# Chained attention and two mixtures of experts: a score burst moved next to another, a first-logits step moved, flags in bf16, prefix counts on TensorE

## The chip, the cores and the metric

One core of one Trainium2 chip runs the whole program. The metric is the device time of one execution in microseconds (us); lower is better. PE is TensorE's matmul side and PEld its weight loads, DVE is VectorE, ACT is ScalarE, POOL is GpSimd, SP is SyncE, which here issues most of the DMAs. PSUM is the memory into which TensorE writes its products.

## The reference

Three layers follow each other. The sizes are batch 8, 8 heads, 576 positions, head size 64, 32 packed queries `p`; 8 experts with 512 inputs and 1024 hidden units.

```python
p_packed = sm_attn(p, k, v)            # softmax(p k^T / 8) v
out = sm_attn(q, p_packed, p_packed)   # softmax(q p_packed^T / 8) p_packed
x = out.transpose(0, 2, 1, 3).reshape(B * S, H * D)
# layer 1: every row goes to its best of 8 experts
idx = argmax(x @ w_gate); g = softmax(x @ w_gate)[idx]
x = g * (relu(x @ w1[idx]) @ w2[idx])
# layer 2: only rows with x @ w_skip > 0, added to x
out = x; out[do] = x[do] + g * (relu(x[do] @ w1[e]) @ w2[e])
```

## The kernel before, in words

The kernel is one program for TensorE above all. For each batch b it has a **main pass** `gen_M(b)` (from line 756): the batch is taken with one expert of layer 1, in two halves of 288 positions. A half is stage 1 (8 hidden blocks f, 6 matmuls each, line 728) and stage 2 (4 output blocks t, 24 matmuls each, line 749). Each product is taken as three matmuls, since both factors are split in a high and a low fp32r part: `hh` (ACT, line 733) and `hl` (DVE, line 734) are the parts of the hidden values, `W2h` and `W2l` those of the second weights, `A2h` and `A2l` those of the attention weights, `Q1h` and `Q1l` those of the first weights multiplied by the packed attention values. An output block t leaves PSUM by ACT (line 765) in the first half and by DVE, times the gates `gB`, in the second (line 767, the *sink*). The second stage of batch 7's first half is gated as well. The rows that belong to another expert than the batch's are done afterwards as *extra units* (`gen_x`, with `x_flags` finding them) and layer 2 as *items* (`e_item`) with a *small unit* beside them (`gen_pick` chooses its rows).

The work of the other batches goes between the steps of the main pass. `Weave` counts the 48 steps of a main pass (one f of stage 1, or 6 matmuls of stage 2) and calls a *side generator* when its place comes: a side is (generator, number of pieces n, a, b) and its pieces stand evenly between the fractions a and b of the pass. A piece that uses TensorE (marked `TE`) is let in only at every fourth step, and only one of each side at a step. So the tuple of numbers sets the order of every engine's queue. The lines that set it in a pass of batch b:

```python
plan = ((NS, 0.06, 0.18, TE), (NT, 0.18, 0.477), (8, 0.5, 1.06))   # b = 1..5
plan = ((NS, 0.06, 0.17, TE), (NT, 0.17, 0.33), (NR, 0.34, 0.52))  # b = 6
sides.append((pre, 5, 0.88, 1.0, TE))
sides.append((w2, 4, 0.76, 1.1))
```

The sides that matter here:

- `gen_S(b+2)`, the **scores**: 16 small matmuls of keys with the packed queries (helper at line 385, output `s`, 64x32 tiles of the array), row maxima `mx` on DVE (line 407), `nm`, four exponentials on ACT (line 417), then the transposes `at` on PE (line 434) of those results, copied by ACT (`aT`).
- `gen_pre(b+1)`: loads of the first weights and the **q products** of them (line 385, output `q`, four PSUM outputs of 128x512, the same 64x32 tiles), each split by ACT (`Q1h`, line 623) and DVE (`Q1l`, line 624).
- `gen_w2(b+1)`: four loads and splits of the second weights (`W2h` on ACT, `W2l` on POOL).
- `gen_R(b)`: the first logits (line 580) and their routing, in the end `csA` (line 588), from which `x_flags` (line 966) finds with 10 fp32 matmuls (line 970) which extra units are needed.
- `gen_post`: the second logits (line 793).

PSUM is one pool of eight banks, handed out in turn (`mt`, line 241): a bank is written again when the product that stood in it eight calls earlier has been read.

At batch 7, `gen_x` prepares an extra unit beside the first half of the main pass: four gate products `xro` on DVE (line 1040), then the transposes `xt` on PE (line 1046). After the second half the program loads the register `cA` (line 1509) in every engine and branches on it.

Of the kernel before, what the change touches and what calls it, by code (L numbers as in the profile page):

```python
# [15 lines left out]
ALU = mybir.AluOpType  # L16
# [102 lines left out]
def attn_moe_kernel(ctx, tc, q, k, v, p, wg, w11, w12, w21, w22, out):  # L119
# [18 lines left out]
    def ct(name, shape, dt=F32, fill=None, eng=None):  # L138
        t = const.tile(shape, dt, name=name)
        if fill is not None:  # L140
            (eng or nc.vector).memset(t, fill)
        return t
# [5 lines left out]
    iot = ct("iot", [128, 128])  # L148
    pid = ct("pid", [128, 1])
    E8 = ct("E8", [128, E])  # L150
    M5 = ct("M5", [128, 5, 2, NXP])
    once = ct("once", [128, 5, 32])
    tri = ct("tri", [128, 128])
    ones = ct("ones", [128, 128])
# [566 lines left out]
    def stage1(lh, ll, rh, rl, kt, hh, hl, hf=None):  # L721
        n_, nr = hh.shape[2], rh.shape[2]
        for f in range(8):
            ps = mt("h")
            n = 0
            for t in range(kt):
                for l, r in ((lh, rh), (lh, rl), (ll, rh)):
                    nc.tensor.matmul(  # L728
                        out=ps[:, 0:nr], lhsT=l[:, t, 128 * f:128 * f + 128], rhs=r[:, t, :],
                        start=(n == 0), stop=(n == 3 * kt - 1),  # L730
                    )
                    n += 1
            nc.scalar.activation(out=hh[:, f, :], in_=ps[:, 0:n_], func=ACTF.Relu)  # L733
            nc.vector.scalar_tensor_tensor(  # L734
                out=hl[:, f, :], in0=ps[:, 0:n_], scalar=0.0, in1=hh[:, f, :].bitcast(F32),
                op0=ALU.max, op1=ALU.subtract,
            )
            if nr > n_:
                nc.vector.tensor_scalar(out=hf[:, f, :], in0=ps[:, n_:nr], scalar1=0.0, scalar2=None, op0=ALU.max)
            yield  # L740
# [224 lines left out]

    def x_flags():
        f0 = mt("f0")
        for z in range(2):
            for s in range(5):
                nc.tensor.matmul(  # L970
                    out=f0[0:NXP, B * z:B * z + B], lhsT=M5[:, s, z, :], rhs=csA[:, s, :], start=(s == 0), stop=(s == 4)
                )
        FL = X["FL"]
        Fv = FL.rearrange("p (b z) -> p b z", z=2)
        nc.vector.tensor_scalar(
            out=Fv, in0=kmA[0:NXP, :].unsqueeze(2).to_broadcast([NXP, B, 2]), scalar1=-1.0, scalar2=float(E),
            op0=ALU.mult, op1=ALU.add,
        )
        nc.vector.tensor_tensor(out=FL, in0=FL, in1=valx[:, :, 2], op=ALU.not_equal)
        nc.vector.scalar_tensor_tensor(  # L980
            out=Fv, in0=f0[0:NXP, 0:2 * B].rearrange("p (z b) -> p b z", z=2), scalar=0.0, in1=Fv,
            op0=ALU.is_gt, op1=ALU.mult,
        )
        nc.tensor.matmul(out=f0[0:32, 64:64 + 2 * B], lhsT=ones[0:NXP, 0:32], rhs=FL, start=True, stop=True)
        nc.vector.tensor_reduce(
            out=X["cnt"], in_=f0[0:32, 64:64 + 2 * B].rearrange("p (b z) -> p b z", z=2), op=ALU.add, axis=AX.X
        )
# [44 lines left out]
                out=EB["W2"][:, :, 128 * t:128 * t + 128], in_=w12[dsn(ex, 1), t].rearrange("o p f c -> p (o f) c")  # L1032
            )

    def gen_x(X):
        li = X["li"]
        A2g, bd, xt, hr, hx, ro, yx = (X[n] for n in ("A2", "bd", "xt", "hq", "hx", "rq", "y"))
        for hp in range(4):
            r = slice(32 * hp, 32 * hp + 32)
            nc.vector.tensor_tensor(  # L1040
                out=bd[r, :, hp, :], in0=A2g[r], in1=X["gB"][r].unsqueeze(1).to_broadcast([32, 2, UW]), op=ALU.mult
            )
        yield
        ps = mt("xt")
        for x in range(2):
# [119 lines left out]

    def gen_pick(d):

        gc, f, cu, po, Og = d["gc"], EB["f"], EB["cu"], EB["po"], EB["O"]
        nc.vector.tensor_scalar(out=f, in0=gc, scalar1=0.0, scalar2=None, op0=ALU.is_gt)
        for j in range(1, 5):  # L1170
            nc.vector.tensor_tensor(out=cu[:, j:j + 1], in0=cu[:, j - 1:j], in1=f[:, j - 1:j], op=ALU.add)
        yield TE
        ps = mt("pk")
        nc.tensor.matmul(out=ps[:, 0:5], lhsT=trib, rhs=f, start=True, stop=False)
        nc.tensor.matmul(out=ps[:, 0:5], lhsT=oneb, rhs=cu[:, 0:5], start=False, stop=True)
        nc.vector.tensor_copy(po, ps[:, 0:5])
        for j in range(5):
            nc.vector.tensor_scalar(
                out=Og[:, j, :], in0=iot, scalar1=po[:, j:j + 1], scalar2=gc[:, j:j + 1],
                op0=ALU.is_equal, op1=ALU.mult,  # L1180
            )
# [178 lines left out]
    for b in range(B):  # L1360
# [4 lines left out]
        if b + 2 <= B:  # L1365
            if b == 0:
                sides.append((part(w20, 2), 2, 0.0, 0.08))
                sides.append((w20, 2, 0.18, 0.32))
                sides.append((part(pre0, 2), 2, 0.03, 0.06))
                sides.append((chain(gen_R(0), pre0, gen_gB(0)), 17, 0.22, 0.36))  # L1370
                sides.append((gate(0, 4), 4, 0.57, 0.7))
            elif b < B - 1:
                sides.append((chain(gen_R(b), gen_gB(b)), 15, 0.06, 0.22))
                sides.append((gate(b, 2), 2, 0.4, 0.48))
            if b + 2 < B:
                if b:
                    plan = ((NS, 0.06, 0.18, TE), (NT, 0.18, 0.477), (8, 0.5, 1.06))
                else:
                    plan = ((2, 0.04, 0.075), (5, 0.115, 0.235), (NT, 0.235, 0.48), (8, 0.5, 1.06))
            else:  # L1380
                plan = ((NS, 0.06, 0.17, TE), (NT, 0.17, 0.33), (NR, 0.34, 0.52))
            sides += [(part(A, n), n, *w) for n, *w in plan]
        if b + 1 < B:
            pre = gen_pre(b + 1)
            w2 = gen_w2(w12, us[b + 1], False)
            sides.append((chain(part(pre, 1), part(w2, 1)), 2, 0.5, 0.6))
            sides.append((part(pre, 2), 2, 0.7, 0.85))
            sides.append((pre, 5, 0.88, 1.0, TE))
            if b + 2 == B:
                sides.append((gen_gB(b + 1), 2, 0.97, 1.0))  # L1390
            sides.append((w2, 4, 0.76, 1.1))
        if b < B - 1:
            W = Weave(gen_M(b), NM, sides, EVERY if b else 2)
        if b == B - 2:
            W.run(0.53)
            run_gen(A)
            a_ctx.close()
            ep = e1_ctx.enter_context(tc.tile_pool(name="ep", bufs=1))
# [13 lines left out]
            X["bd"] = X["ro"][:, 256:512].rearrange("p (x h c) -> p x h c", x=2, c=UW)  # L1412
            X["li"] = xs.tile([1, 3], I32, name="xli")
            cx = X["cx"] = xs.tile([32, 3], F32, name="cx")
            EB["cu"] = xs.tile([128, 5], BF16, name="ecu")
            nc.vector.memset(EB["cu"], 0.0)
            nc.vector.memset(X["bd"], 0.0)
            EB["gc"] = [xs.tile([128, 5], F32, name=f"egc{i}") for i in range(2)]
            EB["gB"] = [xs.tile([128, S], F32, name=f"egB{i}") for i in range(2)]
# [26 lines left out]
        elif b == B - 1:  # L1446
            iA = slice(0, 1)
            d0 = {}

            def load0():  # L1450
                d = dict(EB)
                d["e"] = nc.sync.value_load(lyA[2:3, iA], min_val=0, max_val=E - 1)
                e_load1(d)
                yield
                e_load2(d)
                yield

            def first_half(withx):
                run_gen(expect("none"))
                sides = [(late_post(b - 1), 20, 0.0, 1.0), (load0(), 2, 0.92 if withx else 0.5, 1.0)]  # L1460
                if withx:
                    gx = gen_x(X)
                    sides += [(part(gx, 7), 7, 0.5, 0.8), (gx, 18, 0.8, 1.0)]
                Weave(gen_M(b, (0,)), NM // 2, sides, 1).run()

            xcnt = nc.values_load(cxi[0:1, 0:1], min_val=0, max_val=XB * NXB)
            with tc.If(xcnt == 0, label="nox") as c:
                first_half(False)
            with c.Else():
                first_half(True)  # L1470
            d0.update(e_load(lyA, iA, 0, True, False))
            W = Weave(gen_M(b, (1,)), NM // 2, [])
            W.run(1 / 3)
            q1_ctx.close()
            e2 = ctx.enter_context(tc.tile_pool(name="e2", bufs=1))
            EB["Xh"], EB["Xl"] = (e2.tile([128, 4, S], F32R, name=n) for n in ("eXh", "eXl"))
            EB["W1h"], EB["W1l"] = (e2.tile([128, 4, F], F32R, name=n) for n in ("eW1h", "eW1l"))
            d0.update({n: EB[n] for n in ("Xh", "Xl", "W1h", "W1l")})
            W.add(gen_epre(d0, ("W1", "X")), 8, 0.34, 0.92)
            def early():  # L1480
                yield TE
                us[b]["L"] = mt("L")
                store(b, 0, 8)
                logits(b, 0, 1)
                yield

            W.add(early(), 2, 0.4, 0.6)
            W.run(0.84)
            store(b, 8, NU, 0, 2)
            W.run()  # L1490
        else:
            W.run()
# [13 lines left out]
    EB["hr"] = X["h"]  # L1506
    EB["xT"] = X["ro"].rearrange("p (t c) -> p t c", t=4)
    ds = {}
    cA = nc.values_load(lyA[3:4, 0:1], min_val=0, max_val=1)

    def gen_load(s):
        d = e_load(lyB, slice(s + 1, s + 2), s + 1, True)
# [201 lines left out]
```

## Time and profile before

| | |
|---|---|
| median of 3 runs | 596.32 us (596.19 to 596.82) |
| the profiled execution, whole | 596.14 us |
| its span in the trace | 594.4 us |
| mean granted TensorE clock | 0.998 |
| busy share PE, PEld, DVE, ACT, POOL | 97%, 90%, 57%, 36%, 23% |
| DMA | 123.05 MB, mean 207 GB/s |

The span runs from the first to the last instruction on the core; the whole time has 1.7 us around it. "Busy" is time in which an engine worked at an instruction. The chain that ended last is the list of work, followed back from the last instruction, each step ending what the next one waited for. In a timeline a row gives start, duration, engine, line, operation and out<-in; several instructions of a kind that follow each other without a gap share a row (xN), and a bracket gives the idle time before it and what ended that.

### The profile page before, as it was taken

To read this page: it belongs to the slowest core of one execution; us is meant where nothing else is said; L and a number is where in the kernel's file an instruction comes from. 1 tells how busy PE (TensorE), PEld (TensorE's weight loads), DVE (VectorE), ACT (ScalarE), POOL (GpSimd) and SP (SyncE) were. 2 spreads that over 40 slices of the span, in tenths; PEclk is the share of its full clock that TensorE was granted. 3 is DMA by queue.
4 is the path that set the end of the run, shared out by engine and by line. 5 is a ranking of instruction groups with operands and counts; after the bars stand their busy time and mean duration, and the time that the engine had idled before them with its cause. 6 is when DMAs were issued, how large, how long until landed. Compare 5 with 4: busy or idle time off the path is not lost.

```text
span 594.4 us, 14695 instructions
## 1 busy us (share of the span) xinstructions
PE 578.4 (97%) x5901; PEld 532.2 (90%) x5902; DVE 337.4 (57%) x1001; ACT 216.7 (36%) x475; POOL 135.3 (23%) x122
## 2 busy tenths in 40 slices
PE   7799999999999999999999999999999999999996
PEld 5479899989989989989989898899999999999795
DVE  3878468558638738747746864446846336163110
ACT  3463452542553362344345234224414325052110
POOL 4051331241060150141133105020301220140032
PEclk9999999999999999999999999999999999999999
DMA  8987869567647737826715526996147592722064
GB/s 332 354 320 277 343 243 343 173 242 277 246 171 255 281 148 283 305 74 256 271 41 199 206 71 195 323 320 217 48 132 275 72 374 79 204 53 114 1 99 63
DMA packets 35994, 123.05 MB, mean 207 GB/s; under 512 B 5696, under 2 KB 15680, under 8 KB 29888
## 3 DMA queue, kind: packets, MB, share of 16 engines
q1 hardware_dynamic: 30352, 115.80, 53.2%
q0 software_dynamic: 3968, 4.85, 6.2%
q10 hardware_dynamic: 1584, 1.25, 0.7%
q8 instruction: 50, 0.82, 0.6%
q14 instruction: 40, 0.33, 0.2%
HBM read 92.62 MB, written 29.26 MB: 205 GB/s over the span
## 4 chain that ended last, share of the span: by engine, by line
PE 74%; another core or an unknown queue 6%; DVE 5%; DMA 5%; issue 3%; SPq 2%; ACT 1%; POOL 1%; POOLq 0%; DVEq 0%
PE y L749 30%; PE h L728 23%; PE y L1338 9%; PE s L385 3%; PE q L385 2%; DMA out_dram<-iXR 2%; SPq L1031 1%; DMA gm2d<-gT 1%; PE L L793 1%; PE pv L447 1%; PE at L434 1%; DMA pT<-in_p_dram 1%; DMA egB<-gm2d 1%; PE L L580 1%
## 5 line engine op out<-in xcount | busy, mean ns | idle before, releaser
L749 PE MATMUL y<-hh,W2h 128*128 128x288 f32 x512 | 155.4, 303 | 0.5 <-ACT hh L733 0.5
L749 PE MATMUL y<-hl,W2h 128*128 128x288 f32 x512 | 151.3, 296 | 0.8 <-DVE hl L734 0.6
L749 PE MATMUL y<-hh,W2l 128*128 128x288 f32 x512 | 150.8, 294 | 0.0
L749 PEld LDWEIGHTS y<-hh,W2h 128*128 128x128 f32 x512 | 96.0, 187 | 10.7 <-issue 6.6
L749 PEld LDWEIGHTS y<-hl,W2h 128*128 128x128 f32 x512 | 96.2, 188 | 1.4 <-DVE hl L734 1.4
L624 POOL TENSOR_TENSOR W2l<-W2c,W2h 128x1024 fp32r<-128x1024 f32 x28 | 67.0, 2400 | 131.1 <-ACT W2h L623 112.0
L749 PEld LDWEIGHTS y<-hh,W2l 128*128 128x128 f32 x512 | 96.4, 188 | 0.3 <-issue 0.3
L728 PE MATMUL h<-A2h,Q1h 128*128 128x288 f32 x256 | 77.3, 302 | 2.0 <-DVE T L527 2.0
L734 DVE SCALAR_TENSOR_TENSOR hl<-h,hh 128x288 fp32r<-128x288 f32 x128 | 57.2, 452 | 35.1 <-ACT hh L733 34.1
L728 PE MATMUL h<-A2h,Q1l 128*128 128x288 f32 x256 | 75.5, 296 | 0.0
L728 PE MATMUL h<-A2l,Q1h 128*128 128x288 f32 x256 | 75.3, 295 | 0.0
L733 ACT ACTIVATE hh<-h 128x288 fp32r<-128x288 f32 x128 | 52.3, 413 | 61.3 <-PE h L728 57.0
L728 PE MATMUL h<-eXh,eW1h 128*128 128x288 f32 x192 | 57.7, 300 | 0.7 <-DMA x2d<-y 0.7
L1338 PE MATMUL y<-ihh,iW2h 128*128 128x288 f32 x192 | 56.8, 296 | 0.0
L1338 PE MATMUL y<-ihh,iW2l 128*128 128x288 f32 x192 | 56.6, 295 | 0.0
L728 PE MATMUL h<-eXl,eW1h 128*128 128x288 f32 x192 | 56.5, 295 | 0.0
L1338 PE MATMUL y<-ihl,iW2h 128*128 128x288 f32 x192 | 56.5, 294 | 0.0
L728 PE MATMUL h<-eXh,eW1l 128*128 128x288 f32 x192 | 56.5, 294 | 0.0
L728 PEld LDWEIGHTS h<-A2h,Q1h 128*128 128x128 f32 x256 | 48.0, 187 | 6.1 <-ACT Q1h L623 2.9
L728 PEld LDWEIGHTS h<-A2h,Q1l 128*128 128x128 f32 x256 | 48.1, 188 | 0.6 <-DVE Q1l L624 0.5
L623 ACT CAST W2h<-W2c 128x1024 fp32r<-128x1024 f32 x30 | 31.7, 1055 | 45.4 <-DMA W2c<-in_w_dram 18.3
L728 PEld LDWEIGHTS h<-A2l,Q1h 128*128 128x128 f32 x256 | 48.1, 188 | 0.0
(300 smaller groups left out, 949.8 us busy)
## 6 DMA issues: line engine op xcount, KB each, us to landing
eW<-in_w_dram SPq DMA_DIRECT2D x8, 2048.0 KB
W2c<-in_w_dram SPq DMA_DIRECT2D x30, 512.0 KB
y<-in_w_dram SPq DMA_DIRECT2D x18, 512.0 KB
v<-in_v_dram SPq DMA_DIRECT2D x7, 1280.0 KB
W1c<-in_w_dram SPq DMA_DIRECT2D x16, 512.0 KB
kT<-in_k_dram SPq DMA_DIRECT2D x7, 1152.0 KB
qT<-in_q_dram SPq DMA_DIRECT2D x7, 1152.0 KB
x2d<-y SPq DMA_DIRECT2D x7, 1152.0 KB
```

Source lines behind the costliest of these rows:

```text
L385: m = nc.tensor.matmul(out=out[x][32 * hp:32 * hp + 32], lhsT=lhsT[64 * x:64 * x + 64, 32 * hp:32 * hp + 32], rhs=rhs(hp)[64 * x:64 * x + ...
L434: last = nc.tensor.transpose(ats[x][:, 128 * j:128 * j + 128], a1[:, x, 128 * j:128 * j + 128], ident).ins
L447: nc.tensor.matmul(out=pv[x][32 * hp:32 * hp + 32], lhsT=aT[:, 4 * x + j, 32 * hp:32 * hp + 32], rhs=vm[:, 2 * hp + x, j, :], start=(j == ...
L580: nc.tensor.matmul(out=L[32 * i:32 * i + 32, 0:LN], lhsT=gs[:, g, :], rhs=A2[:, g, c:c + LN], start=(g == 0), stop=(g == 1),)
L623: a = nc.scalar.copy(out=hi, in_=x)
L624: z = eng.tensor_tensor(out=lo, in0=x, in1=hi.bitcast(F32), op=ALU.subtract)
L728: nc.tensor.matmul(out=ps[:, 0:nr], lhsT=l[:, t, 128 * f:128 * f + 128], rhs=r[:, t, :], start=(n == 0), stop=(n == 3 * kt - 1),)
L733: nc.scalar.activation(out=hh[:, f, :], in_=ps[:, 0:n_], func=ACTF.Relu)
L734: nc.vector.scalar_tensor_tensor(out=hl[:, f, :], in0=ps[:, 0:n_], scalar=0.0, in1=hh[:, f, :].bitcast(F32), op0=ALU.max, op1=ALU.subtract,)
L749: nc.tensor.matmul(out=ps[:, 0:HALF], lhsT=l[:, f, :], rhs=r[:, f, :], start=(n == 0), stop=(n == 23))
L793: nc.tensor.matmul(out=L[32 * i:32 * i + 32, 0:LN], lhsT=wgB[:, t, :], rhs=y1[:, t, LC[i]:LC[i] + LN], start=(t == 0), stop=(t == 3),)
L1338: nc.tensor.matmul(out=ps[:, 0:HALF], lhsT=l[:, f, 128 * t:128 * t + 128], rhs=r[:, f, c], start=(n == 0), stop=(n == 23))
```

## The change

1. In the passes of batches 0 to 5, the scores of batch b+2 stand right behind the q products of batch b+1 instead of 72 matmuls ahead of them; the q products begin earlier.
2. In the pass of batch 6, the first logits of batch 7 are one block of 8 matmuls, later.
3. The extra units' flags: `csA > 0` is written as 0 or 1 in bf16 (`csb`, one more DVE instruction), the table `M5` is bf16 too, and the 10 matmuls are of bf16.
4. In batch 7's first half the four gate products of `gen_x` may be issued only after the `hl` that was last written (`us[0]["hl"]`).
5. The loads of the register `cA` stand before the second half of batch 7.
6. In `gen_pick` the running column counts (four dependent DVE additions) go; their matmul is four small bf16 matmuls on the flags.

```diff
@@ stage1
-            nc.vector.scalar_tensor_tensor(
+            ins = nc.vector.scalar_tensor_tensor(
                 out=hl[:, f, :], in0=ps[:, 0:n_], scalar=0.0, in1=hh[:, f, :].bitcast(F32),
...
+            us[0]["hl"] = ins.ins
@@ x_flags
+        nc.vector.tensor_scalar(out=csb, in0=csA, scalar1=0.0, scalar2=None, op0=ALU.is_gt)
...
-                    out=f0[0:NXP, B * z:B * z + B], lhsT=M5[:, s, z, :], rhs=csA[:, s, :], start=(s == 0), stop=(s == 4)
+                    out=f0[0:NXP, B * z:B * z + B], lhsT=M5[:, s, z, :], rhs=csb[:, s, :], start=(s == 0), stop=(s == 4)
@@ gen_x
+        last = tail["hl"] if tail else None
...
+            with tc.issue_after(last) if last is not None else nullcontext():
+                nc.vector.tensor_tensor(
+                    out=bd[r, :, hp, :], in0=A2g[r], in1=X["gB"][r].unsqueeze(1).to_broadcast([32, 2, UW]), op=ALU.mult
+                )
@@ gen_pick
-        for j in range(1, 5):
-            nc.vector.tensor_tensor(out=cu[:, j:j + 1], in0=cu[:, j - 1:j], in1=f[:, j - 1:j], op=ALU.add)
...
-        nc.tensor.matmul(out=ps[:, 0:5], lhsT=oneb, rhs=cu[:, 0:5], start=False, stop=True)
+        for j in range(4):
+            nc.tensor.matmul(
+                out=ps[:, j + 1:5], lhsT=oneb, rhs=f[:, j:j + 1].to_broadcast([128, 4 - j]), start=False, stop=(j == 3)
+            )
@@ the loop over batches
-                    plan = ((NS, 0.06, 0.18, TE), (NT, 0.18, 0.477), (8, 0.5, 1.06))
+                    plan = ((NS, 0.06, 0.18, TE), (NT, 0.18, 0.477), (1, 0.5, 0.57), (7, 0.815, 1.06, TE))
...
-                    plan = ((2, 0.04, 0.075), (5, 0.115, 0.235), (NT, 0.235, 0.48), (8, 0.5, 1.06))
+                    plan = ((2, 0.04, 0.075), (5, 0.115, 0.235), (NT, 0.235, 0.48), (1, 0.5, 0.57), (7, 0.815, 1.06, TE))
...
-                plan = ((NS, 0.06, 0.17, TE), (NT, 0.17, 0.33), (NR, 0.34, 0.52))
+                plan = ((NS, 0.06, 0.17, TE), (NT, 0.17, 0.33), (4, 0.34, 0.41), (NR, 0.45, 0.56))
...
-            sides.append((pre, 5, 0.88, 1.0, TE))
+            sides.append((pre, 5, 0.8, 1.0, TE))
...
-            W.run(0.53)
+            W.run(0.565)
...
-                    gx = gen_x(X)
+                    gx = gen_x(X, us[0])
...
+            cA = nc.values_load(lyA[3:4, 0:1], min_val=0, max_val=1)
             W = Weave(gen_M(b, (1,)), NM // 2, [])
```

How the queues read before and after, at three places. Line numbers of the changed kernel are a little higher (385 is 386, 407 is 408, 728 is 729, 749 is 751).

**PE, the pass of batch 1, from the end of the second half's stage 1.** Here `s` are scores of batch 3, `q` the q products of batch 2, `y` stage 2. Before:

```order
L728 MATMUL h<-A2h,Q1l 128x288
L385 MATMUL s_1741<-kT,pT 32x288
...
L385 MATMUL s_1752<-kT,pT 32x288
L749 MATMUL y<-hh,W2h 128x288
...
L749 MATMUL y<-hh,W2l 128x288
L385 MATMUL q_1887<-W1c,PKT 32x512
...
L385 MATMUL q_1898<-y_1663,PKT 32x512
L749 MATMUL y<-hh,W2h 128x288
```

Now:

```order
L751 MATMUL y<-hh,W2l 128x288
L386 MATMUL q_1813<-W1c,PKT 32x512
...
L386 MATMUL q_1824<-y_1664,PKT 32x512
L386 MATMUL s_1835<-kT,pT 32x288
...
L386 MATMUL s_1846<-kT,pT 32x288
L751 MATMUL y<-hh,W2h 128x288
```

Before, 16 score matmuls stand between stages 1 and 2, then 72 of stage 2, 16 of the q products, 24 of stage 2. Now 48 of stage 2 come first, then the q products and the scores without anything between them, then the other 48.

**ACT, the same pass, after the eight `hh` of that stage 1.** Before:

```order
L417 ACTIVATE a_1802,sm<-s_1741,nm 128x288
L417 ACTIVATE a_1802,sm<-s_1751,nm 128x288
L417 ACTIVATE a_1802,sm<-s_1742,nm 128x288
L417 ACTIVATE a_1802,sm<-s_1752,nm 128x288
L623 CAST W2h<-W2c 128x1024 x3
L623 CAST Q1h<-q_1887 128x512
...
L623 CAST Q1h<-q_1898 128x512
L623 CAST W2h<-W2c 128x1024
L437 COPY aT<-at 128x512 x2
```

Now:

```order
L624 CAST W2h<-W2c 128x1024 x2
L624 CAST Q1h<-q_1813 128x512
...
L624 CAST Q1h<-q_1824 128x512
L418 ACTIVATE a_1898,sm<-s_1835,nm 128x288
...
L418 ACTIVATE a_1898,sm<-s_1846,nm 128x288
L624 CAST W2h<-W2c 128x1024 x2
L438 COPY aT<-at 128x512 x2
```

The exponentials stood ahead of the first three `W2h`; now two `W2h` and the four `Q1h` stand ahead of them.

**DVE, batch 7's first half.** `xro` are the gate products, `hl` the low parts of the hidden values. Before, from the branch on:

```order
L1467 UNCONDITIONAL_BRANCH
L1710 BRANCH_PREFETCH_HINT
L1040 TENSOR_TENSOR xro<-xA_5358,xgB 32x2x32 x4
L1105 TENSOR_LOAD xli
L1105 ISA x2
L734 SCALAR_TENSOR_TENSOR hl<-h,hh 128x288 x2
```

Now, the end of that half's stage 1:

```order
L735 SCALAR_TENSOR_TENSOR hl<-h,hh 128x288
L815 SCALAR_TENSOR_TENSOR fT<-gT,once 128x160
L820 TENSOR_REDUCE csB<-fT 128x1
L735 SCALAR_TENSOR_TENSOR hl<-h,hh 128x288 x2
L1045 TENSOR_TENSOR xro<-xA_5396,xgB 32x2x32 x4
L769 TENSOR_TENSOR y_5358<-y,gB 128x288 x2
```

The four gate products stood ahead of the first `hl` of the half; now they stand behind the last.

## Rows read from the trace of the kernel before

**Rows 1.** The page, part 1: busy us (share of the span), instructions.

```profile
PE 578.4 (97%) x5901; PEld 532.2 (90%) x5902; DVE 337.4 (57%) x1001; ACT 216.7 (36%) x475; POOL 135.3 (23%) x122
```

**Rows 2.** The chain that ended last, batches 2 and 7: start us, us, what.

```profile
156.77 1.13 PE s L385 x32
157.90 9.79 PE y L749 x72
167.70 1.88 PE q L385 x32
169.57 3.39 PE y L749 x24
...
185.12 1.44 PE s L385 x52
...
470.90 25.44 PE h L728 x192
```

**Rows 3.** The chain that ended last, batch 0.

```profile
60.90 1.80 PE h L728 x12
...
72.58 1.88 PE q L385 x32
```

**Rows 4.** PE's timeline, the first eight q matmuls of batch 2's pass.

```profile
167.63 1.09 PE L385 MATMUL q<-W1c,PKT 64*32 64x512 f32 x16
```

**Rows 5.** ACT's timeline, the same pass.

```profile
160.25 0.50 ACT L417 ACTIVATE a<-s,nm 128x288 f32<-128x288 f32 x1 [2.47 <-DVE nm L413]
...
164.45 1.06 ACT L623 CAST W2h<-W2c 128x1024 fp32r<-128x1024 f32 x1 [1.22 <-issue]
...
170.60 2.04 ACT L623 CAST Q1h<-q 128x512 fp32r<-128x512 f32 x4
```

**Rows 6.** DVE's timeline, the same pass.

```profile
158.49 1.54 DVE L407 TENSOR_REDUCE mx<-s 128x1 f32<-128x288 f32 x4
159.95 0.34 DVE L413 TENSOR_SCALAR nm<-mx 128x1 f32<-128x1 f32 x2
...
171.21 2.48 DVE L624 TENSOR_TENSOR Q1l<-q,Q1h 128x512 fp32r<-128x512 f32 x4 [3.02 <-ACT Q1h L623]
```

**Rows 7.** PEld's timeline, batch 6, around the first logits of batch 7.

```profile
328.50 0.19 PEld L749 LDWEIGHTS y<-hh,W2h 128*128 128x128 f32 x1
...
342.58 0.19 PEld L728 LDWEIGHTS h<-A2h,Q1h 128*128 128x128 f32 x1
```

**Rows 8.** DVE's timeline, batch 6: first and last step of that routing.

```profile
339.93 0.35 DVE L281 STREAM_TRANSPOSE LT<-L 128x160 f32<-128x160 f32 x1 [0.60 <-PE L L580]
...
343.28 0.31 DVE L588 TENSOR_REDUCE csA<-gT 128x5 f32<-128x160 f32 x1
```

**Rows 9.** The chain that ended last, batch 6: flags and a small product.

```profile
344.46 1.24 PE f L970 x20
...
358.25 2.59 PE y L749 x18
```

**Rows 10.** DVE's timeline, batch 7's first half.

```profile
369.14 3.14 DVE L1040 TENSOR_TENSOR xro<-xA,xgB 32x64 f32<-32x64 f32 x4 [0.59 <-DVE y L767]
...
377.35 0.81 DVE L734 SCALAR_TENSOR_TENSOR hl<-h,hh 128x288 fp32r<-128x288 f32 x2
```

**Rows 11.** The waits of PEld, 340 to 420 us: total us, times, longest.

```profile
PEld y L749 <- DVE hl L734: 0.9, 1, 0.9
```

**Rows 12.** PEld's timeline, batch 7.

```profile
381.47 0.20 PEld L1046 LDWEIGHTS xt<-xro,xPK 128*64 128x64 f32 x4 [0.16 <-issue]
...
415.63 0.96 PEld L793 LDWEIGHTS L<-y,wgAB 128*32 128x32 f32 x16 [0.16 <-issue]
417.60 0.19 PEld L728 LDWEIGHTS h<-eXh,eW1h 128*128 128x128 f32 x1 [1.01 <-issue]
```

**Rows 13.** Line 1509: duration ns (min/median/max), first and last start.

```profile
L1509 PEldq TENSOR_LOAD <-lyA x1: 468/468/468, 416.3 to 416.3; - x1
```

**Rows 14.** PE's timeline, its last matmul.

```profile
588.27 0.29 PE L1338 MATMUL y<-ihh,iW2l 128*128 128x288 f32 x1
```

More of the change, by code (lines that the diff above doesn't have):

```diff
@@ L150, in attn_moe_kernel @@
     E8 = ct("E8", [128, E])
-    M5 = ct("M5", [128, 5, 2, NXP])
+    M5 = ct("M5", [128, 5, 2, NXP], BF16)
+    csb = ct("csb", [128, 5, B], BF16)
     once = ct("once", [128, 5, 32])
@@ L1033, in x_load, with gen_x @@
             )
-    def gen_x(X):
+    def gen_x(X, tail=None):
         li = X["li"]
+        last = tail["hl"] if tail else None
         A2g, bd, xt, hr, hx, ro, yx = (X[n] for n in ("A2", "bd", "xt", "hq", "hx", "rq", "y"))
@@ L1039, in gen_x @@
             r = slice(32 * hp, 32 * hp + 32)
-            nc.vector.tensor_tensor(
-                out=bd[r, :, hp, :], in0=A2g[r], in1=X["gB"][r].unsqueeze(1).to_broadcast([32, 2, UW]), op=ALU.mult
-            )
+            with tc.issue_after(last) if last is not None else nullcontext():
+                nc.vector.tensor_tensor(
+                    out=bd[r, :, hp, :], in0=A2g[r], in1=X["gB"][r].unsqueeze(1).to_broadcast([32, 2, UW]), op=ALU.mult
+                )
         yield
@@ L1166, in gen_pick @@
     def gen_pick(d):
-        gc, f, cu, po, Og = d["gc"], EB["f"], EB["cu"], EB["po"], EB["O"]
+        gc, f, po, Og = d["gc"], EB["f"], EB["po"], EB["O"]
         nc.vector.tensor_scalar(out=f, in0=gc, scalar1=0.0, scalar2=None, op0=ALU.is_gt)
-        for j in range(1, 5):
-            nc.vector.tensor_tensor(out=cu[:, j:j + 1], in0=cu[:, j - 1:j], in1=f[:, j - 1:j], op=ALU.add)
         yield TE
@@ L1414, in attn_moe_kernel @@
             cx = X["cx"] = xs.tile([32, 3], F32, name="cx")
-            EB["cu"] = xs.tile([128, 5], BF16, name="ecu")
-            nc.vector.memset(EB["cu"], 0.0)
             nc.vector.memset(X["bd"], 0.0)
@@ L1508, in attn_moe_kernel @@
     ds = {}
-    cA = nc.values_load(lyA[3:4, 0:1], min_val=0, max_val=1)
     def gen_load(s):
```

## The prediction

> **What bounds the kernel now.** I read the page's busy shares first: PE is busy 97% of the span and has some 16 us of holes in 594.4, the next engine 57% [rows 1]. So TensorE's queue is the bound, and a change pays as far as it shortens that queue or closes a hole in it. The chain that ended last says the same: stage after stage of matmuls. A long undisturbed stretch gives the price of one matmul, 25.44 / 192 = 0.1325 us [rows 2]; all that a stretch takes beyond that price is what the change can win. I then read what the chain, PEld and the waits show in batches 0, 2, 6 and 7, where queues change. The last matmul starts at 588.27 [rows 14] of 594.4; only the last output's way out follows, which the change leaves alone, so what PE saves earlier arrives at the end.
>
> The profiled execution took 596.14 us, 0.18 below the median of 596.32. The sum is made against the former and the result put on the median. A difference of 0.2% (1.2 us) is about what a measurement of this kernel can tell from none.
>
> **1. The joined burst, six passes.** The score burst takes 1.13 us, and the 72 matmuls behind it 9.79 instead of 9.54, so 1.38 in all. The q burst takes 1.88, and its 24 matmuls 3.39 instead of 3.18, so 2.09 [rows 2]. Both have 32 passes, which differ in columns only (288 and 512), eight passes side by side: (1.88 - 1.13) / (4 x 224) = 0.84 ns a column. By that the scores' columns cost 4 x 288 x 0.84 = 0.96 us and those of q 1.71; the other 0.42 and 0.38 are what it costs to begin and to end a burst. When one stands behind the other, one beginning and one end go. A burst of 52 recorded passes in this trace, of three kinds of product one behind the other, takes 1.44 [rows 2], 0.31 above the 32-pass burst, so a further kind needs no beginning of its own. Take 0.42 x 6 = **-2.5** (0 if a change of product costs the same as a change from the main matmuls; -2.7 if the end shrinks as well).
>
> The join must not add a wait. I replay it from T0, the start of the first q pass, with durations of before. The cast of `W2h` of t = 1 can begin only when the 48th matmul of stage 2 has read the old one (157.90 + 6.36 + 0.2 = 164.45, as its row says [rows 2, 5]), so it runs from T0 + 0.05 to 1.1, at 1.06 us. The first half of q is complete at T0 + 1.1 [rows 4]. ACT then casts `Q1h`, DVE's `Q1l` starts 0.6 later and takes 0.62 each [rows 5, 6], so the first is done at T0 + 2.4 and frees its bank. With four q and four score outputs all eight banks are taken, and the third output block of stage 2 needs that bank at T0 + 1.88 + 0.96 = 2.84: 0.4 us to spare. This is the tightest place. Next, DVE is through with `Q1l` at T0 + 4.2, with the maxima 1.54 later and with `nm` at 6.1 [rows 6]; four exponentials of 0.50 [rows 5] end at 8.1 and the tail copy at 8.4; PE comes to `at` after 48 matmuls, at T0 + 9.4: 1.0 to spare. SP's loads of `kT` and `pT`, which wait for the scores, now stand behind the last two `W2c` loads instead of ahead of them; they are for two batches later, so their delay costs nothing, and the `W2c` loads no longer stand behind that wait. I cost all of this at nothing; were the cover at the banks gone, the price is that of the first rival below.
>
> **2. Batch 0.** There the scores stood 12 matmuls ahead of stage 2's end: 60.90 to 72.58 is 11.68 us for 84 matmuls, at 11.13 [rows 3]. Of the 0.55 above, 0.25 is the burst's end (counted in part 1); 0.30 is a wait behind exponentials that stood ahead of `hh` in ACT's queue and now stand behind. **-0.3** (0 to -0.3).
>
> **3. First logits of batch 7.** Eight small matmuls in three pieces of 2, 4 and 2. From 328.50 to 342.58 [rows 7] is 14.08 us with 90 main matmuls, 11.93; the pieces cost 2.16. As one block they cost one beginning and end, 0.42, and their columns (16 passes of 160, four side by side: 4 x 160 x 0.84 = 0.54): 0.96. **-1.2** (-0.8 to -1.4). They now end later, but 36 main matmuls (4.8 us) follow before the flags; the routing took 343.28 + 0.31 - 339.93 = 3.7 [rows 8], and `csb` adds about 0.2, one more small DVE instruction. 0.9 is left.
>
> **4. Flags.** 20 passes take 1.24 us, 62 ns each [rows 9]; ten bf16 matmuls are ten passes if each is one. **-0.6** (-0.3 to -1.24). 0 and 1 are exact in bf16, so which units are needed stays the same. The small product between 18 matmuls (2.59 instead of 2.39 [rows 9]) now stands with the q burst: **-0.2** (0 to -0.2).
>
> **5. Gate products.** The four `xro` take 3.14 us on DVE ahead of the half's first `hl` [rows 10]; DVE, late from there on, gives the last `hl` at 377.35 + 0.81, and PEld's first stage-2 weights wait 0.9 us for it, the one such wait in that stretch [rows 11]. Without the four ahead, DVE is 3.1 us earlier: **-0.9** (0 to -1.2). They then run behind the last `hl`, from about 376.8 to 379.9; the transposes that read them came at 381.47 [rows 12], now 0.9 earlier at 380.6. The cover is 0.7 us; if it went, the gain would fall by what is lacking.
>
> **6. `cA`.** After batch 7 PEld stands 1.01 us ahead of the first weights of the next item [rows 12]; in there PE's queue loads a register, 0.468 us [rows 13]. The branch stays. The load itself moves between halves, where PE's queue can run ahead of its work. **-0.4** (0 to -0.47).
>
> **7. `gen_pick`.** DVE loses four small additions, which lie beside 97% busy matmuls and are worth nothing, unless the pick waits for them. PE gains three pairs of small passes at 62 ns: **+0.2** (0 to +0.4).
>
> Sum: -2.5 - 0.3 - 1.2 - 0.6 - 0.2 - 0.9 - 0.4 + 0.2 = **-5.9**; 596.14 becomes 590.2 in the trace's execution, and the median **590.4**. All good ends give -7.5, so 588.8; all bad ends -0.7, so 595.6, which needs seven terms to fail together.
>
> **The rivals.**
> *Banks (slower).* The banks come free too late. If the third output of stage 2 waits not for the first `Q1l` but in effect for all four (T0 + 1.76 + 4 x 0.62 = 4.24), PE stands 1.4 us in each pass, 8.4 in all, and the result is 596.3 - 5.9 + 8.4 = 598.8. It decides at 1.0 us a pass, where the six waits eat all 5.9. For it speaks that DVE and ACT must both read every q output and that all eight banks are taken at once; against it the replay, whose slack of 0.4 us would have to turn into a wait of 1.0. Before, `Q1l` waited 3.02 us for ACT [rows 6], which stood in other casts; two of these casts now come later. The Trainium skill speaks for this rival: TensorEngine Tiling (Array Packing), section PSUM Bottleneck, has it that tiling makes TensorE faster but not the emptying of PSUM, so that the copies may become the bottleneck; by it the joined burst would be paced by ACT and DVE and the time would be this rival's 598.8, where the rows above have them ahead by 0.4 us and give 590.4. Chance 0.05.
> *Joining saves nothing.* If the change from q to scores costs as much as a new beginning, part 1 is 0 and the time 592.9. The 52-pass burst speaks against it, though its products are all of 288 columns or fewer. Chance 0.10.
> *Batches 6 and 7 give nothing back.* Their holes may be filled by what comes next: `xt` may wait for the late gate products, the branch for `cA` in another engine, the flags for `csb`. Without parts 5 and 6 and half of part 3 (1.9 together) to all of part 3 (2.5) it is 592.3 to 592.9. Chance 0.09.
> That the change does not do what it says is next to excluded, since the queues show every move.
>
> **How the numbers follow.** The forecast has 0.76 and a range of its own of 589 to 592. The range 588.8 to 593.2 takes in the good ends, both middle rivals and 0.3 for `gen_pick` beyond its term; it leaves out the banks and the mixture of both middle rivals. Faster by over 0.2% needs 1.2 of the 5.9 us: the forecast and both middle rivals give it, 0.95 less 0.02 for their mixture: 0.93. Slower is the banks, 0.04; the same, 0.03, are waits of some 0.8 to 1.2 a pass and the mixture's far end.
>
> **What would show it.** In the chain, one burst of q and scores of some 2.85 us (1.88 + 0.96) where 1.88 and 1.13 stood, and the main matmuls behind it at 0.1325 plus about 0.25 once, with no wait of PE for DVE's `Q1l`. PEld's wait for `hl` near 377 gone and none at `xt`. The flags at about 0.6 us. The stretch with the first logits shorter by 1.2. PEld's hole ahead of the next item at 0.6. I am wrong if the third output of stage 2 waits, or if the joined burst takes 3.2 or more.

## The result, and the profile after

The changed kernel takes **591.48 us** (median of 4 runs, 591.17 to 591.76), the kernel before 596.37 on the same chip; the ratio is 0.9917, with a 95% interval of 0.9900 to 0.9934. It is 4.9 us faster where 5.9 were forecast. The profiled execution has a span of 589.4 us, 5.0 less than before.

Part 1 of the page of the changed kernel, to hold against [rows 1]:

```profile
PE 574.2 (97%) x5894; PEld 532.0 (90%) x5895; DVE 332.5 (56%) x997; ACT 217.4 (37%) x475; POOL 134.6 (23%) x122
```

The chain that ended last in the changed kernel, from the pass that answers to [rows 2]; start us, us, what:

```profile
156.05 6.40 PE y L751 x48
162.45 1.88 PE q L386 x32
164.32 0.97 PE s L386 x32
165.29 6.60 PE y L751 x48
...
342.69 0.32 PE f L973 x10
...
371.52 4.80 PE y L751 x36
376.32 0.37 PE xt L1051 x4
```

Scores behind q cost 0.97 us, which is what their columns were priced at (0.96). The four rows hold 2.85 us of bursts and 0.28 of ends (6.40 + 6.60 less 96 x 0.1325), 3.13 together; the same work took 3.47 before (1.38 + 2.09). The flags fell from 1.24 to 0.32. The second stage of batch 7's first half shows 4.80 us for 36 matmuls, 0.03 over their price, and the transposes `xt` follow it without a gap.

The pieces of the chain that carry the second logits part the passes from each other. Before, then after:

```profile
82.00 1.22 PE L L793 x32
...
129.57 1.22 PE L L793 x32
...
177.14 1.22 PE L L793 x32
...
319.84 1.27 PE L L793 x32
```

```profile
80.85 1.22 PE L L795 x32
...
128.85 1.23 PE L L795 x32
...
176.07 1.22 PE L L795 x32
...
317.71 1.27 PE L L795 x32
...
365.31 1.22 PE L L795 x32
```

A pass took 47.57 us and now takes 47.21 or 47.22, so 0.35 is saved. One pass does not: the one from 80.85 took 48.00, **longer** than before. The rows of the chain inside it name the place, and so does the weight loads' timeline:

```profile
83.73 1.26 PE h L729 x8
85.00 0.54 issue
85.53 2.39 PE h L729 x16
```

```profile
85.53 0.19 PEld L729 LDWEIGHTS h<-A2h,Q1l 128*128 128x128 f32 x1 [0.77 <-issue]
```

PE stands 0.8 us in the middle of a hidden block, after 8 of 24 matmuls, with no wait that the profile knows ("issue"). The trace of before has nothing there. No step of the prediction had this.

By stages, with the difference of the two traces:

| stage | forecast | measured |
|---|---|---|
| six joined bursts, with batch 0's wait (parts 1 and 2) | -2.8 | -2.4 (5 x 0.35, and 0.62 in batch 0) |
| hole in batch 1 | none | +0.8 |
| batch 6: first logits, flags, small product (parts 3 and 4) | -2.0 | -2.2 |
| gate products (part 5) | -0.9 | -0.9 |
| cA (part 6) | -0.4 | 0.0 |
| pick (part 7) | +0.2 | +0.1 |
| the first 43 us, and the way out of the last output | none | -0.3 |

These make -4.9 of the 5.0 by which the spans differ, within rounding. The last line is chance, and here it was luck: in three traces of this kernel the second logits of pass 1 begin between 80.8 and 83.5 us, and all that follows moves along.

### The profile page after: what moved, and what is told of

It is laid out like the page before. It is cut to its first block, busy times and chain, and to the rows that moved or that the text cites. A ratio compares the mean times of both kernels' runs of the same rounds, so it can differ in the third digit from the quotient of the medians.

```text
span 589.4 us, 14689 instructions
## 1 busy us (share of the span) xinstructions
PE 574.2 (97%) x5894; PEld 532.0 (90%) x5895; DVE 332.5 (56%) x997; ACT 217.4 (37%) x475; POOL 134.6 (23%) x122
## 4 chain that ended last, share of the span: by engine, by line
PE 78%; another core or an unknown queue 7%; DMA 5%; DVE 4%; issue 3%; ACT 1%; POOL 1%; POOLq 0%; SPq 0%; DVEq 0%
PE y L751 33%; PE h L729 25%; PE y L1344 9%; PE s L386 3%; PE q L386 2%; DMA out_dram<-iXR 2%; PE L L795 1%; DMA gm2d<-gT 1%; PE pv L448 1%; PE at L435 1%; DMA pT<-in_p_dram 1%; DMA egB<-gm2d 1%; PE L L581 1%; DVE eW1l L625 1%
## 5 line engine op out<-in xcount | busy, mean ns | idle before, releaser
L769 DVE TENSOR_TENSOR y<-y,gB 128x288 f32<-128x288 f32 x48 | 21.6, 449 | 44.4 <-PE y L751 38.9
```

The costliest lines, as they stand in the source:

```text
L769: nc.vector.tensor_tensor(out=y1[:, t, cols], in0=ps[:, 0:HALF], in1=d["gB"][:, cols], op=ALU.mult)
```

## The experiments

Unless a median is given, a comparison is made in the trace, from the second logits of pass 1 on, where runs of one kernel agree within 0.2 us.

**The changed kernel again** (no edit), first in one run, then in five.

> The changed kernel once more, without any edit. Its trace has a hole of 0.77 us in the weight loads at 85.5 us (batch 1, in the middle of an output block, with no wait that the profile shows), and its first 43 us are 0.5 us shorter than before. If the hole belongs to the order of the queues, it is there again at the same instruction, with 0.7 to 0.9 us, and the span is 589.4 +- 0.3; if it was chance, it is gone or elsewhere. If the shorter start is chance, the start differs again by some 0.2 to 0.5 us.

> The changed kernel without any edit, timed beside the next one. 591.5 +- 0.4. The stretch from the second logits of pass 1 to the branch of batch 7 is 284.45 us in its first trace and 284.47 in the second; if both traces tell the kernel's own time, it is 284.4 to 284.5 again, with the hole in batch 1 of 0.75 to 0.85, while the first 81 us differ from run to run.

Measured: the hole is there both times at the same instruction, 0.77 and 0.95 us, so its length differs by more than the 0.75 to 0.85 that was expected. From the second logits of pass 1 to those of batch 7 the three traces took 284.5, 284.5 and 284.6 us. The median of the five runs is 591.81 (591.08 to 591.90) against 596.19. The single run took 593.45, its pass 1 beginning 2.7 us later; its chain has the load of `pT` at 11.93 us instead of 4.89. So the hole belongs to the kernel, and the start to the run.

**The joined burst alone, and everything but it.** The first is the kernel before with the three tuples of numbers changed (the one of batch 0 in the same way as the first one shown); the second is the changed kernel with them put back:

```diff
-plan = ((NS, 0.06, 0.18, TE), (NT, 0.18, 0.477), (8, 0.5, 1.06))
+plan = ((NS, 0.06, 0.18, TE), (NT, 0.18, 0.477), (1, 0.5, 0.57), (7, 0.815, 1.06, TE))
...
-sides.append((pre, 5, 0.88, 1.0, TE))
+sides.append((pre, 5, 0.8, 1.0, TE))
```

> The kernel before with the joined burst alone (part 1 of the prediction, with the earlier q burst). Theory from the two traces: 0.35 us a pass in five passes, 0.6 in batch 0, 0.2 where the small product joins the q burst of batch 6, so 2.6 us; with the hole of 0.8 us in batch 1, which then belongs to it, 1.8. So 594.6 with the hole, 593.8 without. The prediction's own sizes (2.5 + 0.3 + 0.2) would give 593.4. Rival: joining saves nothing, 596.4.

> The changed kernel with scores and q products back at their places of before, all other parts kept. Theory: first logits 1.24, flags 0.92, gate products 0.89, cA nothing, pick -0.07: 3.0 us off the kernel before, 593.4, without the hole in batch 1. Rival: the parts need each other, or the hole comes from elsewhere and stays: 594.2 or more.

Measured: alone, the burst gives 47.22 a pass and a hole of 0.54 in batch 1; its median, 596.10 against 597.85 on a chip where the runs of before spread over 3.8 us (ratio 0.9972, 0.9954 to 0.9991), fits 1.8. Without the burst the passes are 47.55, there is no hole, and the median is 593.09 (ratio 0.9922, 0.9897 to 0.9948); the expected time was 593.4. Against the runs of before on that chip this is 4.8 us, which would leave nothing for the burst; with times that spread so far there, the medians can't settle it, and the passes do. The hole comes with the burst, and the other parts don't need it.

**Scores 24 matmuls ahead of q**, so that two bursts stand apart again, in the plans of batches 0 to 5:

```diff
-(7, 0.815, 1.06, TE)
+(7, 0.72, 1.06, TE)
```

> The changed kernel with the scores 24 matmuls of stage 2 ahead of the q products in the six passes, instead of right behind them; the q products stay where they are. Theory (the joined burst saves one end of a burst, 0.35 us a pass): each of passes 1 to 5 is 0.35 us longer than the 47.21 of the changed kernel, the whole 2.1 us slower, 593.6, less what the hole in batch 1 (0.8) gives if it goes: 592.8. Rival (the saving came from the scores' place in the pass, not from the joint): 47.21 a pass, 591.5.

Measured: the median is 593.68 (593.41 to 594.35). In the chain of this kernel the bursts have their own ends again:

```profile
157.86 3.20 PE y L751 x24
161.05 1.13 PE s L386 x32
162.18 3.38 PE y L751 x24
165.57 1.88 PE q L386 x32
167.44 6.59 PE y L751 x48
```

A pass takes 47.55 (130.66 to 178.21 in the chain), 0.34 more than joined and as long as before. So the joint makes the saving and not the place; the rival that joining saves nothing falls. The hole in batch 1 stayed, 0.76.

**Q1h one cast later.** ACT casts `W2h` of t = 1 twice:

```diff
+            if t == 1 and not early:
+                nc.scalar.copy(out=W2h, in_=W[t])
             split(W2h, W2l, W[t], nc.vector if early and t < 2 else nc.gpsimd)
```

> The changed kernel with the cast of W2h of t = 1 done twice on ACT, so that the four casts of Q1h start 1.05 us later; nothing else. Theory (the replay: the third output block of stage 2 needs the bank 0.4 us after the first Q1l is done): PE waits 0.6 us at that place in each of six passes, 3.7 us in all, 595.2. Rival 1 (no slack at all): 1.05 a pass, 597.8. Rival 2 (the bank does not bind that soon): below 0.3 a pass, 591.5 to 593.

Measured: 594.86 (594.49 to 595.10), 3.4 above the changed kernel; a pass takes 47.77 in its trace instead of 47.21. The weights of the third output block and what they waited for, with the casts of `q` between, first in the changed kernel, then here:

```profile
162.38 0.18 PEld L386 LDWEIGHTS q<-W1c,PKT 64*32 64x32 f32 x16 [0.16 <-issue]
...
163.56 2.05 ACT L624 CAST Q1h<-q 128x512 fp32r<-128x512 f32 x4
...
164.17 1.89 DVE L625 TENSOR_TENSOR Q1l<-q,Q1h 128x512 fp32r<-128x512 f32 x3 [1.23 <-ACT Q1h L624]
...
165.22 0.19 PEld L751 LDWEIGHTS y<-hh,W2h 128*128 128x128 f32 x1 [0.46 <-DVE Q1l L625]
```

```profile
164.25 0.18 PEld L386 LDWEIGHTS q<-W1c,PKT 64*32 64x32 f32 x16 [0.16 <-issue]
...
166.91 1.89 DVE L625 TENSOR_TENSOR Q1l<-q,Q1h 128x512 fp32r<-128x512 f32 x3 [2.10 <-ACT Q1h L624]
...
167.66 0.19 PEld L753 LDWEIGHTS y<-hh,W2h 128*128 128x128 f32 x1 [1.03 <-DVE Q1l L625]
```

From the first q weights to the third block it is 2.84 us, and here 3.41: 0.57 more for a `Q1l` that begins 0.87 later against those weights (2.66 instead of 1.79). The slack was 0.3 to 0.4, and past it every pass pays. The 0.46 that the changed kernel's row puts down to `Q1l` is no cost: the weights stand ready while PE streams the scores, and PE's next matmul begins at 165.29, the end of the burst.

**The stores of batch 0 later.** They are queued on SP behind the store of the gates of pass 1:

```diff
...
+    def late_store(b):
+        with tc.issue_after(gms[1]):
+            store(b, 0, NU)
+        yield
...
-        store(b, 0, NU)
+        if b:
+            store(b, 0, NU)
...
+            if b == 1:
+                sides.append((late_store(0), 1, 0.35, 0.35))
```

> The changed kernel with the two stores of batch 0's result (2.3 MB) queued on SP behind the gates' store of pass 1, some 10 us later. In all traces with the joined burst an instruction fetch of 16 KB (the q8 instruction packets) starts 2.1 to 2.5 us after the second logits' weights in pass 1, where it starts at 0.0 in the trace of before, and PE stands 0.5 to 0.8 us about 1.35 us after its end. Theory (the stores, now issued 1 us earlier against PE, are in the fetch's way): the fetch starts by 1.4 us after those weights, the hole of 0.8 us is gone, 590.7. Rival 1 (another transfer delays the fetch, the load of v for one): fetch and hole stay, 591.5. Rival 2 (the hole is not the fetch's): the fetch moves and the hole stays.

> The kernel with the late stores again, on the same chip as the changed kernel. Theory (its first trace): 0.8 us less than the changed kernel, 590.7 where that has 591.5. Rival: the difference between the two kernels' earlier medians (0.74) came from the chips, and here they are the same.

Measured: no hole, 47.21 in pass 1, and a fetch that starts 1.3 and 1.5 us ahead of the second logits' weights in the two traces. The medians are 590.74 (590.21 to 590.87; ratio 0.9902, 0.9885 to 0.9919) and, on one chip with the changed kernel's 591.81, 590.59 (590.56 to 591.12; ratio 0.9905, 0.9890 to 0.9920). The intervals of the two kernels overlap, yet all comparisons point the same way: 0.7 and, on one chip, 1.2 us in the medians, 0.8 in pass 1 of the trace. It is the fastest version here. The DMA views of the changed kernel, 80.7 to 83.2 us and 83.2 to 84.3, by queue and kind (packets, MB, share):

```profile
q1 hardware_dynamic: 125, 1.00, 99.0%
```

```profile
q1 hardware_dynamic: 39, 0.23, 80.3%
q8 instruction: 1, 0.02, 5.2%
```

And of this kernel, 79.4 to 80.5 us:

```profile
q8 instruction: 1, 0.02, 5.3%
q1 hardware_dynamic: 10, 0.00, 1.3%
```

With the stores the fetch comes after 2.5 us in which the 16 engines carry a full megabyte; without them it comes earlier, through idle engines, and the hole is gone. That the early stores bring both the late fetch and the hole is shown by this: in every trace with the hole they are issued 3.2 us ahead of the second logits' weights, in the two kernels without the joined burst 2.2. That the hole is the fetch's is inferred, since no run moves the fetch alone. For it speak the 1.3 to 1.5 us between the fetch's end and PE's start again, in each kernel with the hole; for the 16 KB being PE's own instructions, that q8 moves 50 such packets in the execution, one to some 240 of the instructions of PE and PEld. What else sets the fetch's place is open: in the changed kernel without the burst the stores stand as in the kernel before, and the fetch starts 1.4 us after those weights instead of 0.0.

**cA's load earlier on PE.**

```diff
+            lds, (cA,) = nc.values_load_multi_w_load_instructions(lyA[3:4, 0:1], min_val=0, max_val=1)
+            ld = [i.ins for i in lds if i.ins.engine == mybir.EngineType.PE][0]
             W = Weave(gen_M(b, (1,)), NM // 2, [])
-            W.run(1 / 3)
+            W.run(1 / 6)
+            with tc.issue_after(ld):
+                W.run(1 / 3)
```

> The changed kernel with PE's load of the register cA forced ahead of the matmuls of the second half's third hidden block; in the changed kernel it still stands right before the branch in PE's queue. Theory (the load is part of the hole at the branch): the stretch from the last logits to the next item's first weights falls from 1.93 us by about 0.4, and nothing opens at the new place; 591.1. Rival 1 (the hole is the branch's own or another engine's, the load lies beside it): the stretch stays at 1.9; 591.5. Rival 2 (the load stops PE's queue wherever it stands): the hole moves, 591.5 with 0.4 more in the middle of the half.

Measured: 591.13 (590.72 to 591.97), not to be told from the changed kernel. The line's view, first of the changed kernel, then here:

```profile
L1476 PEldq TENSOR_LOAD <-lyA x1: 423/423/423, 411.0 to 411.0; - x1
...
L1537 PEldq COMPARE_BRANCH  x1: 330/330/330, 411.6 to 411.6; - x1
```

```profile
L1476 PEldq TENSOR_LOAD <-lyA x1: 317/317/317, 391.5 to 391.5; - x1
...
L1540 PEldq COMPARE_BRANCH  x1: 328/328/328, 412.3 to 412.3; - x1
```

And the weight loads on either side of the branch, of the changed kernel:

```profile
410.41 0.96 PEld L795 LDWEIGHTS L<-y,wgAB 128*32 128x32 f32 x16 [0.16 <-DVE y L769]
412.34 0.19 PEld L729 LDWEIGHTS h<-eXh,eW1h 128*128 128x128 f32 x1 [0.96 <-issue]
```

In the changed kernel the load begins at 411.0, while these 16 weight loads (to 411.37) still run, so all but its tail lies beside them; then come the branch at 0.33 and what follows it. With the load 20 us earlier the stretch from the first of these weights to the item's is 1.81 us; the unedited kernel has 1.93, 1.82 and 1.88 in three traces. The comparison is not quite clean, for here the last of these weights wait for DVE:

```profile
412.33 0.14 PEld L795 LDWEIGHTS L<-y,wgAB 128*32 128x32 f32 x4 [0.22 <-DVE y L769]
413.17 0.19 PEld L729 LDWEIGHTS h<-eXh,eW1h 128*128 128x128 f32 x1 [0.69 <-issue]
```

The hole behind them is 0.69 instead of 0.86 to 0.96, so up to 0.2 us of the load may have been in the way, and not the 0.4 of the theory. Rival 1 is the nearer.

**First logits at the earlier place.**

```diff
-plan = ((NS, 0.06, 0.17, TE), (NT, 0.17, 0.33), (4, 0.34, 0.41), (NR, 0.45, 0.56))
+plan = ((NS, 0.06, 0.17, TE), (NT, 0.17, 0.33), (NR, 0.34, 0.52))
...
-            W.run(0.565)
+            W.run(0.53)
```

> The changed kernel with batch 7's first logits at their earlier place, where the eight matmuls come out in two pieces of 2 and 6 (three of 2, 4 and 2 in the kernel before, one block in the changed). The stretch from the 66th matmul's stage to the next stage 1 took 2.16 us over its 90 main matmuls in three pieces and 0.92 in one. Theory (each piece has its own beginning and end): 1.5 in two. Rival (the place makes it, by a wait for the attention weights): as much as before, 2.1 or more; or 0.9, if the pieces don't matter.

Measured: 1.90 us in two pieces, between the theory's 1.5 and the rival's 2.1 (592.29 in one run). The waits of PEld in that stretch of this kernel name the rest:

```profile
PEld L L581 <- DVE A L551: 0.5, 2, 0.3
```

Of the 0.98 that the place costs over one block, up to half is the wait for the attention weights, which DVE has not turned yet, and the rest the second piece's ends. The first of the two waits (0.33) is hardly longer than the 0.30 that the first piece stands with no wait to its name, so the wait alone may be as little as 0.2. In the same stretch of the kernel before there is one such wait:

```profile
PEld L L580 <- DVE A L550: 0.3, 1, 0.3
```

The prediction had put it all down to the pieces.

**Gate products first.**

```diff
-                    gx = gen_x(X, us[0])
+                    gx = gen_x(X)
```

> The changed kernel with the four gate products of the extra unit ahead of the first hidden values' low parts again. Theory: PE's first stage-2 weights wait 0.9 us for the last of these; the stretch from the second logits of batch 7 to those before the branch is 38.27 as before instead of 37.39, everything else the same: 592.4. Rival (another wait had taken its place, the move alone is worth less): under 0.5 more.

Measured: 592.70 in one run. The stretch of batch 7 is 38.13 instead of 37.39, and PEld's wait is back:

```profile
PEld y L751 <- DVE hl L735: 0.7, 1, 0.7
```

The move is worth 0.7 to 0.9, as its row of before said [rows 11]. Why four products of 32x64 took 3.14 us there [rows 10] is seen in the line's view (ns, min/median/max) of the kernel before, of the changed kernel and of this one, and in POOL's row of the kernel before:

```profile
L1040 DVE TENSOR_TENSOR xro<-xA,xgB x4: 215/220/2444, 369.1 to 372.1; 32x64 f32<-32x64 f32 x4
```

```profile
L1045 DVE TENSOR_TENSOR xro<-xA,xgB x4: 203/218/222, 372.4 to 373.1; 32x64 f32<-32x64 f32 x4
```

```profile
L1045 DVE TENSOR_TENSOR xro<-xA,xgB x4: 211/219/2322, 365.8 to 368.6; 32x64 f32<-32x64 f32 x4
```

```profile
369.13 2.38 POOL L624 TENSOR_TENSOR W2l<-W2c,W2h 128x1024 fp32r<-128x1024 f32 x1 [3.62 <-ACT W2h L623]
```

One of the four lasts 2.44 or 2.32 us instead of 0.22, and it ends 0.07 to 0.08 us after POOL's `W2l`, in both kernels and in the one with the burst alone. In the changed kernel no work of POOL lies there, and the four take 0.95 in all. So most of the 3.14 came from standing beside POOL's work; that it held DVE is inferred from these times, for no run moves POOL's work alone.

## Why the prediction was right, and where it was off

The forecast of a faster kernel held, and 591.48 lies in its range, 1.1 us above the number given. The view that decided was the right one: PE is the bound, and what its queue lost came out at the end. The 0.3 us of the start and the end helped by chance.

- *Joined burst* (-2.5): right in its mechanism, as scores apart by 24 matmuls showed, and too large by 0.4 to 0.5 over the passes. The step took 0.42 for a burst's ends; 0.04 of it was the beginning of the q burst, counted with the 72 matmuls ahead of it, and 0.03 came back at the new end. Measured, 0.35.
- *The replay* held to a tenth: counted from the first q weights, `Q1h` at 1.18 (1.1 in the replay), the first `Q1l` done at 2.4, the third block at 2.84. The slack of 0.3 to 0.4 is real and so is the price behind it, since one more cast on ACT cost 0.57 a pass. The banks' rival didn't come. The Trainium skill has it in TensorEngine Tiling (Array Packing), section PSUM Bottleneck, that emptying PSUM may become the bottleneck once tiling has made TensorE faster. In the changed kernel the trace does not show that, the bank being free 0.3 to 0.4 us ahead of need; in the kernel with one more cast it does, by those 0.57 us.
- *SP's queue* was costed at nothing, and this is the step that the prediction had wrong. It asked who waits for the moved loads' data, and left out the stores. In the changed kernel, not only data had to come through the DMA engines: pass 0's stores began about 1 us earlier against PE's work, a fetch of instructions came late, and PE stood 0.8 us.
- *First logits* -1.2, measured 12.84 us for the stretch instead of 14.08: right in size; up to 0.3 us of it was a wait for the attention weights and not the pieces' ends.
- *Flags* -0.6, measured -0.9: the ten bf16 matmuls are ten passes as forecast, but in the chain a pass takes 32 ns and not the 62 of an fp32 pass.
- *Gate products* -0.9: right. The transposes behind them did not wait; `xt` came at 376.32. The cover is not the 0.7 of the prediction: it took over the 3.14 us to the new place, where the four take 0.95 and end 2.9 us before `xt`.
- *cA* -0.4, measured 0.0: two mistakes. The load did not move in PE's queue, it still stands right ahead of the branch; and at most 0.2 us of it is part of the hole, as moving it showed. The rows of before had this already: the load begins at 416.3 [rows 13], and the weight loads ahead of the hole end at 416.59 [rows 12]. A duration beside a gap was taken for a part of the gap.
- *Pick* +0.2, measured +0.1: three more bf16 matmuls of one pass each, 25 ns apart, and not three pairs at 62.

## What to carry to other kernels

Small tiled bursts between large matmuls cost their columns and, once per burst, a price for their ends (0.35 us here); set them side by side and check by a replay from the trace's own durations that the banks come free in time. When a change shifts large transfers, look in the trace for instruction fetches near them: a bound engine may stand in the middle of a block with no wait to its name. Before a duration is taken to a new place, see whether all instructions of its kind take it: one of the four gate products held nearly all of theirs. A short instruction that seems to lie in a gap is worth nothing until the trace shows that it isn't running beside the work ahead of the gap.

## What was not expected of the hardware

A fetch of 16 KB of instructions took 0.92 to 1.02 us itself, and started up to 2.5 us later than in the kernel before when stores of 2.3 MB were issued 1 us earlier; a hole of 0.54 to 0.95 us on PE followed in every kernel whose fetch started more than 2 us after the second logits' weights of pass 1, and none where it started at 1.4 or 0.0 us after them, or 1.3 to 1.5 ahead. A register load on PE took 0.32 to 0.47 us and ran for the most part beside the weight loads queued ahead of it. One of four DVE products of 32x64 took 2.32 to 2.44 us instead of 0.22 in each of the three kernels in which they began together with a POOL instruction of 2.4 us.
